# Windowed attention and SwiGLU on one core: the first query and key loads regrouped, one store per output tile, one PSUM ring

## The chip, the core and the metric

The kernel runs on one core of a Trainium2 chip. The core has a matrix engine (PE, with its weight loads listed as PEld), three engines for elementwise work (DVE, ACT and POOL), a queue engine (SP) that issues most transfers, and 16 DMA engines. The metric is device microseconds (us) of one launch; smaller is better.

## What is computed

Four batches of eight heads, 768 positions, 64 values per head. Three heads (0, 2, 6) attend to all earlier positions; the other five attend to the first four positions and to the last 64. The attention output, 3072 rows of 512, then goes through a SwiGLU block of width 1536.

```python
scores = scale * np.matmul(q, k.transpose(0, 1, 3, 2))
stream_keep = causal & (is_sink | in_win)
mask = np.where(retr, full_mask, stream_mask)
a = softmax(np.where(mask, scores, -1e9))
x = np.matmul(a, v).transpose(0, 2, 1, 3).reshape(B * S, H * D)
g = x @ w_gate
silu = g * (1.0 / (1.0 + np.exp(-g)))
out = (silu * (x @ w_val)) @ w_out
```

All inputs and the output are float32 in HBM. The kernel casts to float16 on the core and accumulates in float32.

## The kernel before, in words

**Tiles and pairs.** The 3072 rows are 24 tiles of 128 rows. Two neighbouring tiles of a batch are a pair, so there are 12 pairs; `QP` (L150) puts pair 0 of batch 0 and pair 0 of batch 1 first, and these are pairs 0 and 1 of the kernel. For each pair, `load` (L316) brings q, k and v ("x") of 256 rows and all heads as one transfer of 512 KB into a buffer of the ring `raw`: partition p holds rows 2p and 2p+1 of every head, so one contiguous run in HBM is 2 x 64 x 4 = 512 bytes. The weights come the same way in 18 transfers of 512 KB, in runs of 1 KB (gate and value) or 2 KB (output).

**Queries and keys.** `cast` (L382) makes float16 copies in the ring `hq`. For pairs 0 to 4, `transposes` (L415) turns them on PE and `evac` (L423) copies the result from PSUM to `qT` and `kT`; later pairs use a DMA transpose (`dmat`, L408). Within a tile, queries and keys stand with the 64 even rows first and the 64 odd rows after them.

**Attention of a tile.** `scores` (L484) fills a two-bank PSUM buffer of the ring `big` for up to 8 blocks (one unit of `plan`, L441), `exps` (L501) takes the exponential on ACT, `mask` (L510) multiplies by 0/1, `values` (L520) multiplies with v, `norm` (L529) divides. `xtranspose` (L538) turns the tile: for tiles 0 to 7 on PE, for the others by a DMA transpose on SP (L544).

**SwiGLU.** Six groups of four tiles. For each of 12 column blocks, `gate` (L683) makes the gate and the value product in ring `gv`, `tanh` (L691), `stt1` (L695) and `stt2` (L701) combine them into `h`. `outproj` (L717) makes the 512 output columns of one tile with 12 matmuls in three thirds, `oevac` (L728) copies PSUM to an SBUF buffer of ring `osb`, and `store` (L734) writes it out.

**The store.** An output tile stands in SBUF with even rows on partitions 0 to 63 and odd rows on 64 to 127. L739 views the 128 rows in HBM as [2, 64, columns], and L741 to L743 issue one transfer for each half: 64 partitions to 64 rows, 128 KB each. The last tile is cut into 384 and 128 columns, and its second half goes through ACT's queue.

**PSUM.** Eight banks, divided firmly (L167): three single banks `gv`, one `o`, two pairs `big`.

**The order.** Nothing is scheduled at run time. `Plan` (L78) collects some 1020 tasks; the strings `ORDER`, `WAYS` and `SLOTS` (L16 to L62), made beforehand by a planner, say in which order tasks are written to the engines, which engine takes a task that has a choice, and which buffer of a ring it uses. Each engine works through its own tasks in that order. The order also holds filler matmuls (`warm`, L295): ten at the beginning and, in this kernel, 6, 2 and 3 more in gaps of PE before 13 us.

Decoded, SP begins: q0, k0, k1, x0, q1, q2, k2, x1, then weights g1, g0, v1, v0. PE begins: ten fillers, transposes of q0, six fillers, of k0, two fillers, scores of tile 0, and so on; its first SwiGLU product uses g1. PE ends with the four tiles of the last group, 5.0 to 5.3.

Of the kernel before, what the change touches and what calls it, by code (L numbers as in the profile page):

```python
# [16 lines left out]
    "0306070200041I1J1Q1S1R01051K1Lxm1T1U1Vxi1W1X1f1g0A1q1r1z20211d1k1e081N1P1Mxj1Y1Z1a091o1p1w1y0C1O"  # L17
    "1h1i1j2K2Q2R1x2B2C292A2G0D2L2S2T0B1u1t0h22232U2V0g1b1c1m1n0n1s242526138q8r8s8g8h8i1v2D2E2F0y8M8N"
    "8O27280z8W8X2X2Y2f2a2b0m2I2J0F148j8k8Y8t8u8v8w8x0i8y8z8R8S8T2m2j2k2u118Z8a2Z0G2n0o108P8Q8U8V2l8b"
    "8c8d0E2H2y3435169091929596970l2W2p2q0k0I0r2z36370j17939498992M8e8f2N2O0H8l8m8n381l2c2d392e2P1F9U"  # L20
    "9V9W9Z9a9b8o8p2o3B3C3D0J3G3H1C9K9L3e3k3l2g2r2s2v2t0p0q3L3S3T9M0M1G9c9d303V3W199A9B9C3E3F333A3P9X"
    "9Y2h2w2x2i313I3Q3J3M3K3R3f3m3n9P9Q9R1A9D9E3u3v3U3X3Y9F9G9H3N3O323Z3a3b1D9S9T9N9O3r3s0s3o3z3p3c3d"
    "0T9I9JArAsAt0LAmAnAoAcAdAe0t15AfAg0u18ApAq9y9zA0AXAYAZAaAb4243444546470K3h4H4P4O0wAh3g4G4M4NA8A9"
    "AA129eA1A23q3w3t3x403yAuAv0x1HABAC0v1B4D4W4X4T4U4V0Q4w4z4x0N4K4L4IANAOAk9f4JAPAiAjAl0X4Y4Z0P3i48"
    "49A6ASATAU0eA3A4A5A70R1E9g9h9iAL4v52534Q6d3j4A4R4S4B4E4C0O0S9j9k9l9m9n4d4o4p4g4h4iAVAW414F4a4b4c"
    "4f4e0UAIAJAKAQAR4j4k4l4m4n9o9p9q4u514q4rADAE9r9t9u9v9w4yAG505E4s5455564t5O5V0W0c7A0YAFBkAHBlBLBM"
    "AwBmBOBNBPBnBo9x5WAM5N5U5T5B5C6k5D9sBpBqBrBfBgBhC9CACBCCCDC4C5C60VBT5758595A7j7rAxAy5z65AzB05R61"
    "785F5G5K5X5Y5Z5a5i5b5cBiBj606866B1B2B3B45d5e5r5s6eBsBt5H5I5L5J5M6364BuBvBwBzC05l5m5o5p5q5wC162B6"
    "B7B8B9BxBy5QBQBRBSBUBBBC5P5f5g5h5jBVBWBXC2C30Z6f6h6g6i676C6D6E696A5S0bBYBZ6lC7C85n5t5u5v5xBaBbBc"
    "BGBHBIBJBKBdBeBD6H6I5k6F6G6j5yDMDNDOCnCoCpD7D8D9DPDQ6B6J6K6L6NCxCyCzD0D1777E7FBABE6M6S6T6U6X6YCY"  # L30
    "DADB6m6x6n6y6o6pDCDDDEDHDIDJ6u736v6wCZ6O6P6Q6RCECFCGCqCrCaDKDLB5CHCJCKCL6z0dDUDFDGBFCMCO0f7l7kD2"
    "D3D40a6q6r6s7i70717274DRDSDTDVCPCQ767D7C7G7J7K7H7L7ICNCbCc6tCg6V6W7o7p7BCRCSCdCeCiCjCk6Z6a6b6cCI"
    "CTCUCfChCsCtCuCvCw7R7X7U7f7Y7Z7V7WCVCWD57a7b7nD67M7N79ClCm75E0E1E2EAEBECE3E4DqDrDsDtDuEFEGEHEIEJ"
    "EjEkElE5E6E7DvDwE8E9DxEZEa7O7P7Q7SDyDzEbEmEn7q7s7v7w7x7t7uDWDXDYDZDa80817yEeEfEg7c7d7g7e7zDbDcDd"
    "858B8C8D88898AEKELEcEdEN7T7h82838684DeDgDhDi8E8FEMEO8G8HDfEDEPEQER7m8I8J8K8LESETEhEiDjDlDmDnEEEU"
    "EVEWEXEY87FhFiFjFwFxFyFLF8F9FBCXDoDpEoEpEqFAFCFDFIFJErEtEsEuFKFMFNFOFPFQFRFEFFEvFkFlFGFHFmFnFoFc"
    "FdFeFXFYFfFgFZFuEwEyEzExF0F1F2DkFzFrFsF3F4G0FtFvG1G2G3FaFbFSFTFUF5F6F7FVFWFpFqG4G5G6G7G8G9GAGBGC"
    "GDGEGFGGGHGIGLGJGMGNGQGOGKGPGRGS"
)
WAYS = (  # L40
    "000000000000000000000000000000000000000000000000000000000000222222202202212222220200122001100100"
    "000000000000010022112212000011000000100000000000220021010100000100000210000000100000020022122000"
    "000010000000000100100000100000000022100201000010010000022000000000000220222222000000000000000002"
    "100010010000000012222200000010000000000000220012022000000000000000200001000000002202002010000001"
    "000000000010000000000000000120122000000000000000010002002222220000001000000001100000000000001002"
    "222000000000010000000000001001000000000000000000000000000000000000000000000000000000000000000000"
    "000000000000000000000000000000100001000000000000000000000000000000000000000000000000000000000000"
    "000000000100001000010000000000000000000000000000000000000000000000000000000000000000000000000000"
    "000000000000000000000000000000000000000000000000000000000000000000000000010000000000000010000000"
    "000000000000000000000000000000000000000000000000000000000100000000000000100000000000000000000000"  # L50
    "0000000000000000000000000000000000000000000000100000000000010"
)
SLOTS = (
    "0013427562C075931CADB91402567AB9387CD98D834BA1AB6D4285601010010000211011320215122041300240120012"
    "010121051403120120010110402000100513021113401100411020021304001012001511110402101302420100105141"
    "110100213020514011040021015030100511020411310012131200341300140211105020102100311041005120011021"
    "020321020111210100111021222002110002122410015011281112B1020A000291001701126000100012111F1100J012"
    "1H0121M000210011L2021K0021E2010C2101I1121D0000G01000101211091120N10128011261021A1110300110002140"
    "01051121B1100720002000101012010L1112C0000I0111M0011D0101H0122G1020J1002E012012002F2001K000000011"
    "102811120111060012N20217001190012A011222010B001142100521013010101011112C1010D2010I2110L2011E0110"  # L60
    "12011G1102M1100F0022J2021H1122K001100110"
# [57 lines left out]
def kernel(  # L119
# [13 lines left out]
    nc = tc.nc  # L133
# [34 lines left out]
             "h": 2 * NJ, "osb": 2, "gv": 3, "o": 1, "big": 2}  # L168
# [7 lines left out]
    for r in ("raw", "hq", "e", "xb", "xt", "sig", "sil", "h", "osb"):  # L176
        pools[r] = ctx.enter_context(tc.tile_pool(name="p_" + r, bufs=1))
    for r in ("gv", "o", "big"):
        pools[r] = ctx.enter_context(tc.tile_pool(name="ps_" + r, bufs=1, space=PSUM))
# [3 lines left out]
    def buf(ring, shape, dt, name):  # L183
        return pools[ring].tile(shape, dt, name=name, tag=ring + running[-1].slots[ring])
# [92 lines left out]
    kT = [const.tile([128, NT, 2, 2, 128], FH, name=f"kT{n}") for n in range(2)]  # L277
    QB = 3
    qT = [const.tile([128, 2, 2, 2, 128], FH, name=f"qT{n}") for n in range(QB)]
# [35 lines left out]

    def load(kind, n):  # L316
        r = buf("raw", [128, 1024], FP, "raw")
        landed[kind, n] = r
        if kind in "qkx":
            b, pi = QP[n]  # L320
            sl = slice(pi * 256, (pi + 1) * 256)
            nc.sync.dma_start(  # L322
                out=r.rearrange("p (h x) -> p h x", h=H),
                in_={"q": q, "k": k, "x": v}[kind][b, :, sl, :].rearrange(
                    "h (p j) d -> p h (j d)", j=2))
        elif kind == "o":
            nc.sync.dma_start(
                out=r.rearrange("p (a n) -> p a n", a=2), in_=wod[:, 2 * n:2 * n + 2, :])
        else:
            nc.sync.dma_start(  # L330
                out=r.rearrange("p (a n) -> p a n", a=4),
                in_=(wgd if kind == "g" else wvd)[:, :, n * 256:(n + 1) * 256])

    T_load, T_iss = {}, {}
    for kd, n in ([(kd, n) for n in range(NP) for kd in "qkx"]
                  + [(kd, n) for kd in "gvo" for n in range(6)]):
        T_iss[kd, n] = P.add(f"load {kd}{n}", ["SP"], (lambda kd=kd, n=n: load(kd, n)),
                             takes=["raw"])
        T_load[kd, n] = P.lands(T_iss[kd, n])
# [52 lines left out]
    def castv(n, m, j):  # L392
# [8 lines left out]
             r[m * 64:(m + 1) * 64, :, j].rearrange("p (a c e) d -> p a c e d", a=2, c=2))  # L401

# [160 lines left out]
    def tasks_of_pair(n):  # L563
# [4 lines left out]
        for kd in "qk":  # L568
            cs[kd] = []
            for x in range(2) if n < 2 else [None]:  # L570
# [14 lines left out]
        for kd in "qk":  # L585
# [10 lines left out]
            for x, ps in enumerate([slice(1, 4, 2), slice(0, 4, 2)] if n < 2 else [slice(0, 4)]):  # L596
                T_ev[n, kd].append(P.add(
                    f"ev{kd}{n}.{x}", ["ACT", "DVE"],
                    (lambda n=n, kd=kd, x=x, ps=ps: evac(n, kd, x, ps)), deps=[tr] + old))
# [3 lines left out]
    def tasks_of_tile(t):  # L603
# [3 lines left out]
        k_deps = [x for kt in range(i // 2 + 1) for x in T_ev[QP.index((b, kt)), "k"]]  # L607
        k_deps += T_ev[n, "q"]
# [8 lines left out]
        for u, unit in enumerate(units):  # L617
# [4 lines left out]
                       deps=k_deps + k_sinks + added, takes=["big"])  # L622
# [51 lines left out]

    for n in range(NP):
        tasks_of_pair(n)
        tasks_of_tile(2 * n)
        tasks_of_tile(2 * n + 1)
# [29 lines left out]
    def pieces(g, tt):  # L708
# [4 lines left out]
        if tt < SIZES[g] - 1:  # L713
            return [(("o", "big", "big")[tt], 0, DM)]
# [11 lines left out]
    T_oe = {}  # L726
# [7 lines left out]
    def store(g, tt, x):  # L734
# [5 lines left out]
        final = g == NG - 1 and tt == SIZES[g] - 1  # L740
        for j in range(2):  # L741
            eng = nc.scalar if j and final else nc.sync
            eng.dma_start(out=rows[j], in_=o_sbs[g, tt][j * 64:(j + 1) * 64, lo:hi])  # L743

    for g in range(NG):
# [29 lines left out]
        for tt in range(SIZES[g]):  # L775
            stores = []
            for x, (ring, lo, hi) in enumerate(pieces(g, tt)):
                for third in range(3) if x == 0 else [0]:
# [9 lines left out]
                    for j in range(js.start, js.stop):  # L788
# [5 lines left out]
                st = P.add(f"st{g}.{tt}.{x}", ["SP"], (lambda g=g, tt=tt, x=x: store(g, tt, x)),  # L794
                           deps=[oe], after=stores[:1])
# [45 lines left out]
```

## Time and profile before

| what | value |
|---|---|
| median of 3 runs | 257.44 us (255.44 to 258.09) |
| profiled execution | 254.62 us, its span 252.8 us |
| PE busy | 242.1 us, 96% of the span |
| DVE, ACT, POOL busy | 161.5, 133.9, 90.1 us |
| granted PE clock, mean | 0.997 |
| DMA, whole span | 40.72 MB, mean 161 GB/s |
| first score matmul of queries and keys | 9.27 us |
| first SwiGLU matmul | 21.62 us |
| last matmul ends | about 248.6 us |

The span runs from the first to the last instruction of the profiled execution; 1.8 us of its time lie outside it. In the groups of the profile [...]groups of matmuls add up by their busy time, not by count times mean. "DMA share" is the mean busy share of the 16 DMA engines; it exceeds 1 where packets overlap on an engine.

### The profile page before, as it was taken

To read this page: it belongs to the slowest core of one execution; us is meant where nothing else is said; L and a number is where in the kernel's file an instruction comes from. 1 tells how busy PE (TensorE), PEld (TensorE's weight loads), DVE (VectorE), ACT (ScalarE), POOL (GpSimd) and SP (SyncE) were. 2 spreads that over 40 slices of the span, in tenths; PEclk is the share of its full clock that TensorE was granted. 3 is DMA by queue.
4 is the path that set the end of the run, shared out by engine and by line. 5 is a ranking of instruction groups with operands and counts; after the bars stand their busy time and mean duration, and the time that the engine had idled before them with its cause. 6 is when DMAs were issued, how large, how long until landed. Compare 5 with 4: busy or idle time off the path is not lost.

```text
span 252.8 us, 5192 instructions
## 1 busy us (share of the span) xinstructions
PE 242.1 (96%) x2009; PEld 124.7 (49%) x2009; DVE 161.5 (64%) x291; ACT 133.9 (53%) x212; POOL 90.1 (36%) x118
## 2 busy tenths in 40 slices
PE   7987999999999979999999999999999999999993
PEld 3566755654545534444555445544455544444442
DVE  2666888877877654866887655676863556563610
ACT  3666888867686415768445843664354411232010
POOL 7376889965291703810650230500134100000000
PEclk9999999999999999999999999999999999999998
DMA  6999999999996988996954757441014131114133
GB/s 182 290 308 334 319 334 315 330 324 178 325 290 142 231 184 211 207 180 133 187 66 87 208 145 93 96 87 19 0 28 68 35 83 41 41 33 95 41 85 85
DMA packets 73369, 40.72 MB, mean 161 GB/s; under 512 B 25600, under 2 KB 68864, under 8 KB 73344
## 3 DMA queue, kind: packets, MB, share of 16 engines
q1 hardware_dynamic: 73184, 40.25, 69.1%
q8 instruction: 16, 0.26, 0.4%
q10 hardware_dynamic: 160, 0.13, 0.2%
q14 instruction: 9, 0.07, 0.1%
HBM read 28.31 MB, written 6.29 MB: 137 GB/s over the span
## 4 chain that ended last, share of the span: by engine, by line
PE 79%; DMA 8%; SPq 6%; POOL 3%; issue 1%; DVE 1%; ACT 1%; ACTq 0%; POOLq 0%; DVEq 0%
PE gv L687 46%; PE o_ps L722 22%; PE sc L499 5%; SPq L322 4%; PE av L526 4%; DMA raw<-in_moe_w_gate_dram 3%; DMA xt<-xb 3%; DMA qT<-hq 2%; POOL wg_sb L192 1%; SPq L743 1%; PE xtr L550 1%; PE tr L420 1%; DVE xb L534 1%; POOL e L516 1%; ACT sig L693 0%
## 5 line engine op out<-in xcount | busy, mean ns | idle before, releaser
L507 ACT ACTIVATE e<-sc 128x1024 f16<-128x1024 f32 (+2 forms) x68 | 59.5, 907 | 31.0 <-PE sc L499 29.1
L697 DVE SCALAR_TENSOR_TENSOR sil<-sig,gv 128x512 f32<-128x512 f32 (+1 forms) x76 | 49.8, 657 | 36.4 <-ACT sig L693 35.2
L687 PE MATMUL gv<-xt,wg_sb 128*128 128x512 f16 (+1 forms) x304 | 70.8, 368 | 1.7 <-POOL wg_sb L192 1.4
L687 PE MATMUL gv<-xt,wv_sb 128*128 128x512 f16 (+1 forms) x304 | 71.5, 368 | 0.5 <-POOL wv_sb L192 0.4
L693 ACT ACTIVATE sig<-gv 128x512 f32<-128x512 f32 (+1 forms) x76 | 43.3, 576 | 53.0 <-PE gv L687 52.3
L722 PE MATMUL o_ps<-wo_sb,h 128*128 128x512 f16 (+2 forms) x300 | 67.0, 371 | 0.0
L704 DVE SCALAR_TENSOR_TENSOR h<-sil,gv 128x512 f16<-128x512 f32 (+1 forms) x76 | 49.2, 656 | 16.7 <-PE gv L687 14.6
L516 POOL TENSOR_TENSOR e<-e,m 128x640 f16<-128x640 f16 (+1 forms) x16 | 28.2, 1769 | 44.5 <-ACT e L507 44.2
L722 PEld LDWEIGHTS <-h 128*128 128x128 f16 x300 | 28.2, 98 | 31.8 <-issue 0.2
L687 PEld LDWEIGHTS <-wv_sb 128*128 128x128 f16 x304 | 28.4, 98 | 31.0 <-POOL wv_sb L192 0.5
L687 PEld LDWEIGHTS <-wg_sb 128*128 128x128 f16 x304 | 27.7, 98 | 30.5 <-POOL wg_sb L192 1.7
L192 POOL CAST vt<-raw 64x512 f16<-64x512 f32 x30 | 19.7, 659 | 28.2 <-DMA raw<-in_v_dram 26.9
L499 PE MATMUL sc<-qT,kT 64*128 64x128 f16 x472 | 21.8, 218 | 1.8 <-DMA qT<-hq 1.7
L499 PEld LDWEIGHTS <-kT 64*128 64x128 f16 x472 | 14.4, 94 | 16.7 <-issue 15.5
L526 PEld LDWEIGHTS <-e 128*128 128x128 f16 x472 | 17.0, 97 | 5.0 <-issue 1.1
L516 DVE TENSOR_TENSOR e<-e,m 128x1024 f16<-128x1024 f16 (+1 forms) x22 | 14.3, 648 | 7.8 <-ACT e L507 7.5
L190 ACT COPY o_sb<-o_ps 128x512 f32<-128x512 f32 (+1 forms) x14 | 8.1, 578 | 21.0 <-PE o_ps L722 19.2
L526 PE MATMUL av<-vt,e 128*128 128x65 f16 x472 | 18.2, 193 | 0.5 <-POOL vt L192 0.2
L192 POOL CAST hq<-raw 128x1024 f16<-128x1024 f32 (+1 forms) x17 | 16.4, 972 | 5.0 <-DMA raw<-in_q_dram 3.3
L534 DVE TENSOR_TENSOR xb<-av,rc 128x512 f16<-128x512 f32 x24 | 16.6, 691 | 1.5 <-DMA xt<-xb 0.7
L192 DVE COPY o_sb<-o_ps 128x512 f32<-128x512 f32 (+1 forms) x11 | 7.2, 651 | 13.0 <-PE o_ps L722 13.0
L192 POOL COPY vt<-vt 2x330 f16<-2x330 f16 x10 | 4.5, 452 | 19.9 <-PE av L526 19.5
(42 smaller groups left out, 111.9 us busy)
## 6 DMA issues: line engine op xcount, KB each, us to landing
raw<-in_q_dram SPq DMA_DIRECT2D x12, 512.0 KB, 7.3
raw<-in_k_dram SPq DMA_DIRECT2D x12, 512.0 KB, 7.2
raw<-in_v_dram SPq DMA_DIRECT2D x12, 512.0 KB, 7.2
out_dram<-o_sb SPq DMA_DIRECT2D x46, 128.0 KB, 2.4
raw<-in_moe_w_gate_dram SPq DMA_DIRECT2D x6, 512.0 KB, 8.3
raw<-in_moe_w_val_dram SPq DMA_DIRECT2D x6, 512.0 KB, 8.1
raw<-in_moe_w_out_dram SPq DMA_DIRECT2D x6, 512.0 KB, 6.2
xt<-xb SPq DMA_TRANSPOSE x16, 2.8
```

Source lines behind the costliest of these rows:

```text
L192: ENG[task.way].tensor_copy(out=dst, in_=src)
L322: nc.sync.dma_start(out=r.rearrange("p (h x) -> p h x", h=H), in_={"q": q, "k": k, "x": v}[kind][b, :, sl, :].rearrange("h (p j) d -> p h ...
L499: nc.tensor.matmul(sc[:, c:c + n, :], weights, moving, start=first, stop=last)
L507: nc.scalar.activation(out=e[:, at], in_=whole_sc.pop((t, u))[:, at], func=AF.Exp, scale=scale)
L516: ENG[task().way].tensor_tensor(out=ev, in0=ev, in1=mm, op=ALU.mult)
L526: nc.tensor.matmul(avs[t][:, odd, n * 66:n * 66 + 65], ee, vv, start=(m == 0), stop=(m == len(bl) - 1))
L534: nc.vector.tensor_tensor(out=xb.rearrange("p n o d -> p o n d"), in0=av[:, :, :, 0:64], in1=rc.to_broadcast([128, 2, 4, 64]), op=ALU.mult)
L687: nc.tensor.matmul(ps, wsb[:, kk, j * 128:(j + 1) * 128], xt[:, kk, c[0]:c[1]], start=(kk == 0), stop=(kk == 3))
L693: nc.scalar.activation(out=sg[g, j, c], in_=gs[g, j, c], func=AF.Tanh, scale=0.5)
L697: nc.vector.scalar_tensor_tensor(out=sl[g, j, c], in0=sg.pop((g, j, c)), scalar=1.0, op0=ALU.add, in1=gs.pop((g, j, c)), op1=ALU.mult)
L704: nc.vector.scalar_tensor_tensor(out=hs[g, j][:, c[0]:c[1]], in0=sl.pop((g, j, c)), scalar=0.5, op0=ALU.mult, in1=vs.pop((g, j, c)), op1=A ...
L722: nc.tensor.matmul(o_open[g, tt, x], hs[g, j][:, tt * 128:(tt + 1) * 128], wo_sb[:, j, lo:hi], start=(j == 0), stop=(j == NJ - 1))
```

## The change

It does five things.

1. Queries and keys of pairs 0 and 1 come in eight transfers of 256 KB (`load_odds`), four with the odd heads first, then four with the even heads. Each fills 32 partitions: q0 on partitions 0 to 31, k0 on 32 to 63, q1 on 64 to 95, k1 on 96 to 127. A partition holds 8 rows of a head, a run of 2 KB. All four share the buffers 0 to 3 of `raw`.
2. One cast then takes a pair of heads of all four tensors at once (`cast4`, four casts of 1024 columns instead of eight of 512), `transposes4` turns it with 8 transposes, as many in all as before, and `evac4` copies it in two parts, one for each pair of tiles. A score unit waits only for the heads that it uses.
3. `store` issues one transfer for a tile, with the HBM side [2, 64, columns] and the SBUF side [128, columns]. It may go through SP's or ACT's queue. `osb` has three buffers.
4. The eight PSUM banks are one space; a slot number names a bank, and a `big` buffer takes two neighbouring ones. `raw` and `hq` are each one tensor that is cut into slots.
5. The order, the engines and the slots are planned anew. There are no fillers after the first ten.

Decoded from the new strings, SP begins: k1, q0, k0, q1 (odd heads), k0, q0, q1, k1 (even heads), x0, k2, q2, x1, v0, g0, g1, v1. PE begins: ten fillers, the transposes of the odd heads (`tr4.3`, `tr4.2`), of the even heads, score units 1.0, 0.0, 1.1, 3.0, 2.0; its first SwiGLU product uses v0, after `xe0` and `xe1`. PE ends: out 4.1, four products of group 5 and value and gate products, out 4.2, the first third of out 4.3, out 5.0, 5.1, 5.2, 5.3 (384 columns, then 128), the last two thirds of out 4.3. The last stores are 4.1 (ACT), 4.2, 5.0, 5.1 (SP), 5.2 (ACT), 5.3 in two parts (SP, ACT) and 4.3 (ACT). Around 80 to 110 us SP holds: xdma8, dq7, xdma9, load q9, dk6, load k8, stores 0.1 and 0.2, load k7, dq8.0, xdma10, store 1.0, xdma11, dk7, with store 0.0 on ACT's queue ("xdma" turns a finished tile, "dq" and "dk" are the DMA transposes of queries and keys).

```diff
     RINGS = {"raw": 14, "hq": 5, "e": 6, "xb": 3, "xt": 2, "sig": 2, "sil": 3,
-             "h": 2 * NJ, "osb": 2, "gv": 3, "o": 1, "big": 2}
+             "h": 2 * NJ, "osb": 3, "ps": 8, "gv": 8, "o": 8, "big": 8}
...
-    for r in ("gv", "o", "big"):
-        pools[r] = ctx.enter_context(tc.tile_pool(name="ps_" + r, bufs=1, space=PSUM))
+    banks = [psum.tile([128, 1024], FP, name=f"banks{x}") for x in range(4)]
+    rooms = {"raw": const.tile([128, RINGS["raw"], 1024], FP, name="rooms_raw"),
+             "hq": const.tile([128, RINGS["hq"], 1024], FH, name="rooms_hq")}
...
+    def load_odds(kind, n, odd):
+        b, pi = QP[n]
+        at = 64 * n + 32 * "qk".index(kind)
+        nc.sync.dma_start(
+            out=rooms["raw"][at:at + 32, 0:4].rearrange("p a b -> p (a b)").rearrange(
+                "p (h o x) -> p h o x", o=2, x=512)[:, :, odd],
+            in_={"q": q, "k": k}[kind][b, :, pi * 256:(pi + 1) * 256, :].rearrange(
+                "(h o) (p j) d -> p h o (j d)", o=2, j=8)[:, :, odd])
...
+    def cast4(p):
+        src = rooms["raw"][:, 0:4].rearrange("p a b -> p (a b)").rearrange(
+            "p (k s r j d) -> p k s r j d", k=2, s=2, r=2, d=64)
+        hqs[p] = buf("hq", [128, 1024], FH, "hq")
+        recast(T_c4[p], hqs[p].rearrange("p (j s d) -> p s j d", s=2, d=64),
+               src[:, p % 2, :, p // 2])
+
+    def transposes4(p):
+        tr = trs[p] = buf("gv", [128, 8, 128], FH, "tr")
+        for j in range(8):
+            nc.tensor.transpose(
+                tr[:, :, j * 16:j * 16 + 16],
+                hqs[p][:, j * 128:(j + 1) * 128], ident)
+
+    def evac4(p, x):
+        at = p % 2 * 256 + p // 2 * 128
+        dst = qkT[:, 2 * x:2 * x + 2, 0:1024].rearrange("c g (m n) -> c g m n", m=2)
+        copy(T_e4[p, x], dst[:, :, :, at:at + 128].rearrange(
+                 "c g m (i n l) -> c g m i n l", i=2, l=4),
+             trs[p].rearrange("c (x g m) (l i n) -> c x g m i n l", x=2, g=2, i=2, l=4)[:, x])
...
         rows = out[r0:r0 + 128, lo:hi].rearrange("(p j) n -> j p n", j=2)
-        final = g == NG - 1 and tt == SIZES[g] - 1
-        for j in range(2):
-            eng = nc.scalar if j and final else nc.sync
-            eng.dma_start(out=rows[j], in_=o_sbs[g, tt][j * 64:(j + 1) * 64, lo:hi])
+        eng = nc.scalar if T_st[g, tt, x].way == "ACT" else nc.sync
+        eng.dma_start(out=rows, in_=o_sbs[g, tt][:, lo:hi])
```

## The prediction, made before the result was known

> **What bounds the kernel now.** First the page: its head, the slices of PE and DMA, and the chain of waits by line.
>
> ```profile
> span 252.8 us, 5192 instructions
> ...
> PE   7987999999999979999999999999999999999993
> ...
> DMA  6999999999996988996954757441014131114133
> ...
> PE gv L687 46%; PE o_ps L722 22%; PE sc L499 5%; SPq L322 4%; PE av L526 4%; DMA raw<-in_moe_w_gate_dram 3%; DMA xt<-xb 3%; DMA qT<-hq 2%; POOL wg_sb L192 1%; SPq L743 1%; PE xtr L550 1%; PE tr L420 1%; DVE xb L534 1%; POOL e L516 1%; ACT sig L693 0%
> ```
>
> PE is full from about 25 us to the end. So the end is: when PE gets full, plus the matmuls left, plus PE's gaps, plus what follows the last matmul. How much gap there is says the table of windows; its columns are PE, PEld, DVE, ACT, POOL busy, clock, DMA share, GB/s.
>
> ```profile
> 25.50:238.00 212.50, 210.03 (x1705) 106.45 (x1705) 145.83 (x251) 117.47 (x189) 74.22 (x82) 1.00 0.68 152
> ```
>
> 2.5 us are idle in the middle; no more can be won there, save on switches between kinds of matmul. The list of waits names for PE only small ones, none on an engine that empties PSUM:
>
> ```profile
> PE sc L499 <- DMA qT<-hq: 1.7, 2, 1.5
> ...
> PE gv L687 <- POOL wg_sb L192: 1.4, 1, 1.4
> ```
>
> Then the chain in order of time, for when PE gets full and for the end:
>
> ```profile
> 12.01 8.39 DMA raw<-in_moe_w_gate_dram
> 20.45 0.08 issue
> 20.53 1.05 POOL wg_sb L192
> 21.57 0.05 issue
> 21.62 1.05 PE gv L687 x8
> ...
> 238.21 10.40 PE o_ps L722 x60
> ...
> 248.64 0.29 DVE o_sb L192
> ```
>
> The first SwiGLU product waits for the ninth 512 KB load (g1), which lands at 20.45. The load stream sets this, as one-microsecond windows show:
>
> ```profile
> 10.00:11.00 1.00, 1.00 (x18) 0.60 (x16) 0.73 (x2) 1.00 (x2) 0.57 (x1) 1.00 1.19 289
> ...
> 17.00:18.00 1.00, 1.00 (x19) 0.83 (x19) 0.23 (x3) 1.00 (x2) 0.30 (x1) 1.00 1.15 345
> ```
>
> DMA is saturated in both: at 289 GB/s with 512-byte runs (q, k, v), at 345 with 1 KB runs (weights). The stores, from the table of transfers and half-microsecond windows of the tail:
>
> ```profile
> out_dram<-o_sb SPq DMA_DIRECT2D x46, 128.0 KB, 2.4
> ```
>
> ```profile
> 245.00:245.50 0.50, 0.50 (x4) 0.25 (x3) 0.00 (x0) 0.00 (x0) 0.00 (x0) 1.00 0.46 111
> 245.50:246.00 0.50, 0.50 (x5) 0.21 (x3) 0.00 (x0) 0.00 (x0) 0.00 (x0) 1.00 1.02 229
> 246.00:246.50 0.50, 0.50 (x5) 0.30 (x4) 0.00 (x0) 0.44 (x1) 0.00 (x0) 1.00 0.83 188
> ```
>
> A tile of 256 KB (two transfers) leaves in about 1.2 us over 16 engines, and each transfer lands 2.4 us after its issue.
>
> [...]a tile stored by two 64-partition transfers averages 262 KB / 1.2 us, about 215 GB/s, though single windows are above it. [...]The trace shows the half clock at the beginning (fillers 0.43 us apart until 5.67, then 0.22) and keeps PE busy afterwards.
>
> **Change 1 and 2, the start.** 2.1 MB of q and k now pass at 290 GB/s: 7.2 us. If run length decides, they pass at 347 (weights): 6.0 us, a gain of 1.2. [...]I take 215, since eight transfers queue without gaps: 9.8 us, a loss of 2.5. v0 has the ninth place that g1 had, so it lands at 20.45 + 2.5 = 23.0; its half cast takes 0.6 instead of 1.05, and the first product starts at 23.7, 2.1 later.
>
> The attention chain must be no later. Data flows from 2.4 us on; the odd half (1.05 MB) lands at 2.4 + 4.9 + 0.9 (what q0 took beyond its flow) = 8.2, the even half at 13.1. Cast of 1024 columns on ACT or POOL 1.1, transposes of two casts 1.1, two evacuations on ACT 2 x 0.58, scores 0.4: unit 0.0 is done at 16.9 (before: 9.9). Then ACT has ex0.0, ex1.1, ex3.0, ex2.0 (4 x 1.03), evk2 (1.02), ex3.1 (1.03), xe0 and xe1 (0.4 each), which ends at 23.9, when PE may start vals0.0. Both chains say 24, against 21.6: +2.4. The casts (4 x 1.04 for 8 x 0.62) and evacuations (8 for 8) save 0.8 us of engine time under the load stream: nothing. Evacuations read PSUM in strides, which no row shows: 0 to 0.4 us each, two on the chain; I take 0.
>
> Eleven fillers go (about 2.9 us of PE, in gaps): no gain. Without them PE idles from 5.7 to about 9.4. If the clock halves, score units take 0.8 instead of 0.4[...]; I take 0.3. Start: **+2.7**, from -1.6 to +4.5.
>
> **Change 3, the store.** HBM [2, 64, 512] has slowest dimension 2, SBUF [128, 512] has 128[...]: each of two engines moves 131,072 bytes, where it moved 16,384. No row shows a single engine alone. [...]from above: the saturated weight stream, 347 / 16 = 21.7 GB/s, 6.0 us. I take 5.3 us, an estimate. All stores, of both queues, share these two engines. Counting from PE's end E, with 0.86 us for four matmuls of 512 columns and 0.6 for the copy, stores are issued at -12.4 (4.2), -8.9 (5.0), -6.3 (5.1), -3.7 (5.2), and the data starts 1.2 later (before: the last ones issued at 248.95, bytes from about 250.1). 4.2 flows until -5.9; from there the two engines are never free: 5.0 until -0.6, 5.1 until 4.7, 5.2 until 10.0, 5.3 (192 and 64 KB) until 15.3, 4.3 until 20.6. The copy of 4.3 also waits for its `osb` buffer until 5.1 has landed, about 6, which is early enough. The span ends 1.5 after the last byte (before: 251.3 to 252.8): 22.1 instead of 252.8 - 248.6 = 4.2. Tail: **+18**, from +13[...] to +22 (6.0). The 25 issues that are saved (about 0.6 us each) lie on SP, which waits for copies there (55 us before L743 in the list of SP's waits): nothing; were SP late, it would be up to 15 us of earlier loads.
>
> Middle: between 80 and 160 us DMA packets take this share of the 16 engines (the table of transfers of that window):
>
> ```profile
> q1 hardware_dynamic: 30969, 12.54, 79.9%
> ```
>
> That is 64 us of 80, perhaps 53 without overlap (saturation showed 1.2). Eight stores add 8 x 5.3 = 42 us to two engines, and every load and transpose needs all 16: 95 to 106 us of work in 80. xdma10 and xdma11 stand on SP behind stores 0.1, 0.2 and 1.0, and gate2.0 waits for them; dk7 after them feeds tile 14. On ACT's queue stand store 0.0 and, behind it, a cast and exponentials of tile 10[...]. The late transposes cost PE between 0 (slack hides it) and 26; from 160 us on the DMA share is 0.23, and it recovers. I take **+6**.
>
> **Change 4 and 5.** PE waits for no PSUM buffer now, so the common ring gives at most part of the 2.5 us idle: -1 to 0, taken as 0. One tensor for all slots could bring waits where slots overlap in the tracking; nothing in the code makes them overlap in bytes: 0. The third `osb` buffer is spent on late stores.
>
> **Sum.** 254.6 + 2.7 + 18 + 6 = 281.3 against the profiled execution. The median of the runs shown is 257.4, 2.8 higher; so half of that is added: 283.
>
> **Rivals.** (A) The main case[...]: 283; its own range 266 to 303. (B) A transfer is divided by its bytes, not by its outermost dimension: the store spreads over 16 engines, and only the slow start counts: the last store is one of 256 KB after a copy of 0.58, some 0.7 later than now; 254.6 + 2.7 + 0.7 - 1 = 257, up to 261 with the median's excess. For it: nothing in the trace[...]. (C) The other side, faster: as B for the stores, and run length, not partitions, decides the rate of the eight quad loads. Place: the load stream until v0; price: -1.2 at 347 GB/s and -0.45 for the shorter cast, with ring and order up to -2.5: 250 to 254. For it: the trace's own step from 289 to 345 GB/s with longer runs. It decides from 290 GB/s on, where the start stops being later. Even then it wins only while a store lands fast: PE makes the last tiles 2.6 us apart, so from 2.6 us per store on the tail piles up, and 5.3 is twice that.
>
> **Chances.** A 0.70, B 0.13, C 0.14, others 0.03. About 1% is what a measurement of this kernel can tell. A is slower; B is half within 1%, a third slower; C is faster: faster 0.17, same 0.09, slower 0.74. Range: A up to 299 (0.65), B (0.12) and C's upper end (0.04) from 253 on.
>
> **What would show it.** A: DMA share near 2/16 with some 40 to 55 GB/s after the last matmul, 18 us of it; issue to landing of a store 7 us or more; landings of xdma10 and xdma11 above 8 us; PE gaps at 90 to 160. B: windows of 200 GB/s and less in the first 12 us, v0's product after 23 us, and a tail of 5. C: over 300 GB/s from the first quad on. Wrong altogether if score units start before 10 us and stores land within 3.

## The result and the profile after

| kernel | median, us | range, us | ratio to before [95% interval] |
|---|---|---|---|
| before | 256.97 (4 runs) | 255.44 to 258.09 | |
| after | 415.46 (4 runs) | 414.54 to 416.11 | 1.617 [1.608, 1.627] |

The change costs 158.5 us. Medians here and below are over all executions; the ratios leave out the few that ran more than 1.5% slower than the fastest of the same kernel. The forecast was 283 us with a range up to 299: the sign was right, the size far too small. The profiled execution took 414.99 us, its span 413.2. First the same rows of the page as before: head, busy times, the slices of PE, its clock and DMA, and the chain by line.

```profile
span 413.2 us, 5149 instructions
...
PE 278.8 (67%) x1998; PEld 136.2 (33%) x1998; DVE 168.7 (41%) x282; ACT 141.5 (34%) x218; POOL 88.1 (21%) x117
...
PE   5867668765678974689757747654948786679710
...
PEclk9599979988889978899998996989896999788975
DMA  8999995062049979157995084100175100000111
...
PE banks L774 30%; DMA out_dram<-o_sb 12%; PE banks L809 9%; DVE sil L784 8%; DVE h L791 7%; ACT sig L780 5%; PE banks L580 3%; ACT e L588 3%; PE banks L607 2%; DMA rooms_raw<-in_k_dram 2%; DMA xt<-xb 2%; SPq L490 1%; ACT o_sb L211 1%; DVE xb L615 1%; DVE e L597 1%
```

PE was full and is now idle for a third of the span, from end to end and not just in the middle or the tail. It also has more busy time (278.8 against 242.1 us) for fewer matmuls: its clock is granted only in part (mean 0.887, before 0.997), and each matmul lasts longer (a gate product 403 ns on average in its group, 368 before). Of the 160.4 us by which the span grew, 36.7 are such busy time; the rest is waiting. New links stand in the chain: `sil`, `h` and `sig`, DVE's and ACT's work on a SwiGLU block, on which PE did not wait before. The list of waits (total, times, longest) says the same:

```profile
PE banks L774 <- DVE sil L784: 38.3, 29, 3.1
...
PE banks L774 <- DVE h L791: 28.6, 21, 3.6
...
ACT o_sb L211 <- DMA out_dram<-o_sb: 23.0, 3, 9.6
...
DVE o_sb L213 <- DMA out_dram<-o_sb: 12.9, 3, 6.7
```

Two groups: SwiGLU products wait for the engines that empty PSUM, and the copies of the output wait for stores. The first group comes earlier than any store. The first store is issued at 128.6 us, but the windows (PE, PEld, DVE, ACT, POOL busy, clock, DMA share, GB/s) show PE at 73% from 40 us on:

```profile
40.00:80.00 40.00, 29.21 (x309) 16.42 (x309) 24.58 (x44) 19.34 (x31) 15.11 (x20) 0.91 0.73 216
100.00:120.00 20.00, 14.56 (x64) 5.67 (x63) 9.69 (x17) 7.67 (x12) 2.12 (x1) 0.83 0.07 12
```

In the second row even DMA is idle (12 GB/s), and no engine is full: a chain of waits, not an engine, sets the pace. The timeline shows one link of it:

```profile
43.49 0.68 DVE L784 SCALAR_TENSOR_TENSOR sil<-sig,banks 128x512 f32<-128x512 f32 x1
...
44.22 1.02 PE L774 MATMUL banks<-xt,wg_sb 128*128 128x512 f16 x4 [1.57 <-DVE sil L784]
```

The four matmuls write bank 0; the DVE instruction that they wait for reads bank 1, decoded from the slots. The two banks have nothing in common but the tensor: the change cuts PSUM into four tensors of two banks each.

The tail is close to the forecast. After the last matmuls only stores run, at a DMA share near 2/16 and 51 GB/s:

```profile
396.00:400.00 4.00, 0.00 (x0) 0.00 (x0) 0.00 (x0) 0.00 (x0) 0.00 (x0) 0.75 0.13 51
404.00:408.00 4.00, 0.00 (x0) 0.00 (x0) 0.00 (x0) 0.00 (x0) 0.00 (x0) 0.50 0.14 49
```

A share of 0.13 to 0.14 is 2.1 to 2.2 of 16 engines. If two engines carry the stores, an estimate from this share, 51 GB/s are 25.5 GB/s an engine, and 262,144 bytes take 5.15 us (forecast: 5.3). The stores of both queues share this rate: one issued on SP at 384.69 us and one on ACT at 387.45 landed together, at 401.7 and 401.9.

### The profile page after: what moved, and what is told of

Its sections match the earlier page's. It is cut to its first block, busy times and chain, and to the rows that moved or that the text cites. A ratio compares the mean times of both kernels' runs of the same rounds, so it can differ in the third digit from the quotient of the medians.

```text
span 413.2 us, 5149 instructions
## 1 busy us (share of the span) xinstructions
PE 278.8 (67%) x1998; PEld 136.2 (33%) x1998; DVE 168.7 (41%) x282; ACT 141.5 (34%) x218; POOL 88.1 (21%) x117
## 4 chain that ended last, share of the span: by engine, by line
PE 46%; DVE 18%; DMA 16%; ACT 10%; issue 4%; SPq 2%; POOL 1%; ACTq 0%; DVEq 0%; POOLq 0%
PE banks L774 30%; DMA out_dram<-o_sb 12%; PE banks L809 9%; DVE sil L784 8%; DVE h L791 7%; ACT sig L780 5%; PE banks L580 3%; ACT e L588 3%; PE banks L607 2%; DMA rooms_raw<-in_k_dram 2%; DMA xt<-xb 2%; SPq L490 1%; ACT o_sb L211 1%; DVE xb L615 1%; DVE e L597 1%
## 5 line engine op out<-in xcount | busy, mean ns | idle before, releaser
L774 PE MATMUL banks<-xt,wg_sb 128*128 128x512 f16 (+1 forms) x304 | 82.2, 403 | 49.4 <-DVE sil L784 22.6
L774 PE MATMUL banks<-xt,wv_sb 128*128 128x512 f16 (+1 forms) x304 | 80.5, 398 | 37.6 <-DVE sil L784 15.7
L780 ACT ACTIVATE sig<-banks 128x512 f32<-128x512 f32 (+1 forms) x76 | 43.4, 575 | 139.3 <-PE banks L774 127.7
L784 DVE SCALAR_TENSOR_TENSOR sil<-sig,banks 128x512 f32<-128x512 f32 (+1 forms) x76 | 49.6, 659 | 84.6 <-ACT sig L780 78.4
L809 PE MATMUL banks<-wo_sb,h 128*128 128x512 f16 (+2 forms) x300 | 73.0, 398 | 15.8 <-DVE h L791 6.0
L588 ACT ACTIVATE e<-banks 128x1024 f16<-128x1024 f32 (+2 forms) x68 | 58.9, 910 | 44.9 <-PE banks L580 34.4
L791 DVE SCALAR_TENSOR_TENSOR h<-sil,banks 128x512 f16<-128x512 f32 (+1 forms) x76 | 49.9, 658 | 46.7 <-PE banks L774 38.1
L597 POOL TENSOR_TENSOR e<-e,m 128x1024 f16<-128x1024 f16 (+1 forms) x17 | 32.8, 1935 | 131.6 <-ACT e L588 131.3
L580 PE MATMUL banks<-qkT 64*128 64x128 f16 x472 | 21.6, 230 | 0.0
L607 PE MATMUL banks<-vt,e 128*128 128x65 f16 x472 | 20.1, 200 | 2.1 <-DVE vt L217 1.6
L213 POOL CAST rooms_hq<-rooms_raw 128x1024 f16<-128x1024 f32 x13 | 13.8, 1060 | 25.5 <-DMA rooms_raw<-in_k_dram 13.2
```

Of the source, the lines that this page charges most:

```text
L213: ENG[task.way].tensor_copy(out=dst, in_=src)
L580: nc.tensor.matmul(sc[:, c:c + n, :], weights, moving, start=first, stop=last)
L588: nc.scalar.activation(out=e[:, at], in_=whole_sc.pop((t, u))[:, at], func=AF.Exp, scale=scale)
L597: ENG[task().way].tensor_tensor(out=ev, in0=ev, in1=mm, op=ALU.mult)
L607: nc.tensor.matmul(avs[t][:, odd, n * 66:n * 66 + 65], ee, vv, start=(m == 0), stop=(m == len(bl) - 1))
L774: nc.tensor.matmul(ps, wsb[:, kk, j * 128:(j + 1) * 128], xt[:, kk, c[0]:c[1]], start=(kk == 0), stop=(kk == 3))
```

## The experiments

The theory after the result: the loss is the sum of (P) waits between neighbouring banks of one PSUM tensor, (S) the store on two engines, and a small rest from the start. The rivals: only one of the two; or the new order itself. "Both" below means that the edits are made together. All medians stand beside runs of the kernel before on the same chip (254.7 to 255.4 us).

| run | edit | median, us | ratio to before [95%] |
|---|---|---|---|
| b_pairs | before, four two-bank tensors | 355.13 | 1.395 [1.389, 1.402] |
| t_half | before, two four-bank tensors | 570.63 | 2.229 [2.212, 2.245] |
| b_one | before, one eight-bank tensor | 254.88 | 1.001 [0.997, 1.004] |
| a_banks | after, eight one-bank tensors | 317.08 | 1.245 [1.241, 1.250] |
| a_one | after, one eight-bank tensor | 313.35 | 1.227 [1.221, 1.233] |
| a_store | after, two stores a tile | 376.95 | 1.482 [1.475, 1.489] |
| a_both | a_banks and a_store | 259.91 | 1.018 [1.012, 1.025] |
| b_store | before, one store a tile | 315.28 | 1.238 [1.233, 1.242] |
| b_store_osb6 | b_store, six output buffers | 300.81 | 1.179 [1.172, 1.186] |
| b_tail | b_store in the last group only | 269.08 | 1.055 [1.050, 1.060] |
| b_mid | b_store in groups 0 to 4 only | 301.03 | 1.182 [1.176, 1.189] |
| b_store16 | before, one store to 128 rows in a row | 251.51 | 0.987 [0.984, 0.990] |
| b_nat | b_store16 with strided moving operands | 404.30 | 1.583 [1.576, 1.591] |
| a_fixed | a_one and the edit of b_nat | 404.80 | 1.586 [1.578, 1.594] |
| b_order | b_store16, rows put in order by DVE | 252.28 | 0.990 [0.987, 0.993] |
| a_order | a_one and the edit of b_order | 256.29 | 1.003 [1.000, 1.005] |
| a_warm | a_order with fillers in the start | 257.00 | 1.008 [1.005, 1.011] |

**PSUM alone, in the kernel before (b_pairs).** Every bank keeps its number; only the tensors are made differently.

```diff
-        pools[r] = ctx.enter_context(tc.tile_pool(name="ps_" + r, bufs=1, space=PSUM))
+    banks = [psum.tile([128, 1024], FP, name=f"banks{x}") for x in range(4)]
...
+            room = banks[at // 2][:, at % 2 * 512:(at % 2 + wide) * 512]
```

> The kernel before; its PSUM buffers keep their banks and their order, but the three gv banks and the o bank are cut out of two tensors of two banks (gv0 with gv1, gv2 with o); each big pair is a tensor as it was. Theory (waits are set for a whole PSUM tensor, so neighbours in one tensor wait for each other): PE waits before products for the reader of the neighbouring bank; slower by 40 to 120 us, the granted clock below 0.95. Rival (the loss comes from the stores or from the new order): within 3 us of before.

It costs 100 us, and the new waits are those of the changed kernel. The granted clock fell less than expected (0.974 in the profiled execution). From the list of waits of this run:

```profile
PE banks L703 <- DVE sil L713: 37.0, 37, 2.3
```

**Is it any shared tensor? (b_one, t_half.)** The same kernel with one tensor of eight banks, then with two of four.

```diff
+    banks = [psum.tile([128, 4096], FP, name=f"banks{x}") for x in range(1)]   # b_one
+    banks = [psum.tile([128, 2048], FP, name=f"banks{x}") for x in range(2)]   # t_half
```

> The kernel before with all eight PSUM banks in one tensor; banks, slots and order unchanged. Theory (a wait is set for any two accesses of one tensor, whatever bank): far slower than with pairs, 420 us and more, since then scores, products and output products exclude each other too. Rival (only the neighbouring bank of a pair counts): about the 355 of pairs.

This missed altogether: one tensor costs nothing. So "a wait for any two accesses of one tensor" fell, and t_half asked whether a larger tensor is harmless or only one that holds all eight banks.

> The kernel before, with its eight banks as two tensors of four banks each (bank numbers unchanged). Theory (waits for neighbouring banks in a tensor of two or four banks): at least as slow as with four tensors of two banks, 355 us; I expect 360 to 450, and waits of PE for the readers in nearly every product. Rival (it is the placing of the buffers in pairs, not the size of the tensor, and a larger tensor is harmless as one of eight banks was): 254 to 257.

Four banks in a tensor are far worse than two: 570.6 us. The list of waits again names the readers:

```profile
PE banks L703 <- DVE sil L713: 69.8, 48, 2.7
...
PE banks L703 <- DVE h L720: 33.4, 40, 2.3
```

With two or four banks in a tensor (355.13 and 570.63 us) a write to one waits for a reader of another; with all eight in one (254.88 us) it does not. The kernels b_pairs, t_half and b_one give every buffer the same bank number and differ only in the tensor that holds it. So which bank a buffer has does not decide, and the waits are most likely set when the program is built; that is argued from these three runs, not read from its instructions. Why a tensor of all eight banks is free of them stays open.

**PSUM and stores undone in the changed kernel (a_banks, a_one, a_store, a_both).** a_banks gives each bank its own tensor, and so cuts the exponentials and the division of `norm` at the bank border; a_one only makes one tensor of the four. a_store issues two transfers a tile, as before.

```diff
-    banks = [psum.tile([128, 1024], FP, name=f"banks{x}") for x in range(4)]
+    banks = psum.tile([128, 4096], FP, name="banks")            # a_one
...
-        eng.dma_start(out=rows, in_=o_sbs[g, tt][:, lo:hi])     # a_store
+        for j in range(2):
+            eng.dma_start(out=rows[j], in_=o_sbs[g, tt][j * 64:(j + 1) * 64, lo:hi])
```

> The changed kernel with each PSUM bank a tensor of its own; an exponential over two banks and the division become two instructions each. Stores as changed. Theory (whole-tensor waits): PE idles little again, 275 to 295 us, which is the store's tail plus the later start. Rival (the new order itself is bad, or the stores are): above 350.

> The changed kernel with its eight PSUM banks as one tensor instead of four tensors of two banks; the store stays one transfer over two engines. Theory (the slow part of the PSUM change is the two-bank tensor, in which a write of one bank waits for a reader of the other; one tensor of eight banks has no such waits): 310 to 325 us, as with a tensor for each bank. Rival (in this kernel, with its buffers spread over all banks, one tensor brings neighbours' waits too): 410 or more.

> The changed kernel with two stores of 64 partitions per tile again, on the queue that the plan names. Theory (PSUM tensors are the main cost, stores only the tail and some waits for output buffers): 415 minus 22 to 45 us, 370 to 393. Rival (stores on two engines are the main cost): 250 to 290.

> The changed kernel with each PSUM bank a tensor of its own (exponentials and divisions in two instructions) and two stores of 64 partitions per tile. What is left of the change: the regrouped loads, the later start without fillers, the new order. Theory (PSUM tensors and stores are all of the loss): 252 to 264 us. Rival (the new order costs by itself): 270 and more.

Either way of mending PSUM gains about 100 us (98.4 and 102.1), as much as b_pairs lost. Two stores gain 38.5 while PSUM is slow and 57.2 once it isn't (317.08 to 259.91): some 19 us are lost as long as either cause is there, so a slow kernel hides part of the late stores. With both, 4.8 us above before are left. a_banks missed its range, since the store's cost was still thought smaller than it is.

**The store alone, in the kernel before (b_store).**

```diff
-        for j in range(2):
-            eng = nc.scalar if j and final else nc.sync
-            eng.dma_start(out=rows[j], in_=o_sbs[g, tt][j * 64:(j + 1) * 64, lo:hi])
+        nc.sync.dma_start(out=rows, in_=o_sbs[g, tt][:, lo:hi])
```

> The kernel before with one store per tile, [2, 64, columns] against [128, columns], all on SP; nothing else. Theory (two engines per store, 5.15 us for 256 KB at 51 GB/s): the tail grows by 16 to 20 us and late transposes cost 0 to 6: 273 to 283 us. Rival (the stores also cause the losses of the middle): 330 us and more.

It costs 60.6 us, over twice what the theory (and the prediction, 24) gave it, and less than the 75 of the rival. The list of waits shows full output buffers:

```profile
ACT o_sb L190 <- DMA out_dram<-o_sb: 49.7, 10, 9.7
...
DVE o_sb L192 <- DMA out_dram<-o_sb: 30.7, 7, 9.5
```

Were these buffers the reason, more of them should win most of it back.

```diff
-             "h": 2 * NJ, "osb": 2, "gv": 3, "o": 1, "big": 2}
+             "h": 2 * NJ, "osb": 6, "gv": 3, "o": 1, "big": 2}
```

> The kernel before with one store per tile, and six output buffers in place of two. Theory (of the 60 us of one store per tile some 40 are copies that stand on ACT and DVE until a slow store gives its buffer back): 272 to 285 us, of which the tail is 18 to 22. Rival (the middle is lost to transposes that are late behind stores on two DMA engines): 300 and more.

They win back 14.5 us, and the waits for stores shrink to one:

```profile
ACT o_sb L190 <- DMA out_dram<-o_sb: 8.2, 1, 8.2
```

Yet the time stays at 300.8. The chain in order of time of that run (start, duration) shows what is late instead: loads and DMA transposes behind the stores.

```profile
113.54 8.94 DMA raw<-in_k_dram
...
147.24 9.31 DMA kT<-hq
...
161.93 9.60 DMA raw<-in_q_dram
...
185.79 10.43 DMA xt<-xb
```

The table of transfers of the kernel before has these medians from issue to landing:

```profile
raw<-in_k_dram SPq DMA_DIRECT2D x12, 512.0 KB, 7.2
...
xt<-xb SPq DMA_TRANSPOSE x16, 2.8
kT<-hq SPq DMA_TRANSPOSE x14, 3.5
```

So the transposes are late above all.

**By stage (b_tail, b_mid).** One transfer for the last group only, or for all groups but the last.

```diff
+        if g == NG - 1:        # b_mid: g < NG - 1
+            nc.sync.dma_start(out=rows, in_=o_sbs[g, tt][:, lo:hi])
+            return
```

> The kernel before; only the four tiles of the last group leave in one transfer over two engines (on SP), the other twenty in two halves as before. Theory (the tail alone): +18 us, 270 to 276. Rival (a good part of what the single stores cost came later through the loads and transposes only, and the tail hides behind the last matmuls): 256 to 265.

> The kernel before; the twenty tiles of groups 0 to 4 leave in one transfer over two engines, the four of the last group in two halves as before. Theory (single stores cost 60.6 us in all, of which 18 are the tail; the rest is late transposes and loads and full output buffers in the middle, and the terms add): 293 to 300. Step of the prediction (middle +6, at most 26): 257 to 281.

The tail costs 14.3 us, the middle 46.2, and together 60.5 they are the whole of b_store. Both runs lie 1 us outside the range of their theory (270 to 276, 293 to 300), and the 257 to 281 that the prediction's step gave b_mid are far off. The windows of b_mid show where:

```profile
80.00:100.00 20.00, 14.82 (x147) 7.71 (x146) 9.16 (x14) 5.66 (x10) 4.96 (x5) 0.96 1.24 158
...
120.00:140.00 20.00, 16.25 (x122) 7.99 (x121) 11.22 (x20) 11.26 (x18) 3.91 (x4) 0.83 0.89 128
...
180.00:200.00 20.00, 11.74 (x93) 5.41 (x91) 6.76 (x13) 7.02 (x12) 2.82 (x5) 0.85 0.61 66
```

and the kernel before in the last of them:

```profile
180.00:200.00 20.00, 20.00 (x192) 10.39 (x191) 11.33 (x21) 8.75 (x12) 7.28 (x8) 1.00 0.22 41
```

PE loses 8.3 us of 20 there while the mean DMA share is 0.61 and only 66 GB/s pass. Single DMA engines are not seen in the profile, but the traces have the semaphore events of the transfers. The kernel before has 2,368 for 148 transfers, half stores among them, 16 for each; the changed kernel has 1,707, which are 16 for each of 102 loads and transposes and 3 for each of 25 stores. Of the three of the store issued at 384.69 us one came at 385.62 and two at the end, at 401.58 and 401.71. With a share of 0.13 to 0.14 in the tail this reads as transfers that need all sixteen engines and wait for the two that the stores keep busy; that is argued from these counts, no engine was seen by itself. The stores hold up the output too: over the run the copies of ACT and DVE stand 39.8 and 21.9 us for output buffers. And 12.5 us of the 46.2 are longer busy time of PE (254.6 against 242.1 us), at a mean clock of 0.951.

**Is it the outermost dimension? (b_store16.)** One store again, but to 128 rows in a row, so that both sides have 128 outermost.

```diff
-        rows = out[r0:r0 + 128, lo:hi].rearrange("(p j) n -> j p n", j=2)
+        rows = out[r0:r0 + 128, lo:hi]
```

> The kernel before with one store per tile, but from 128 partitions straight to 128 rows of HBM, so both sides have an outermost dimension of 128. The same bytes in the same 128 runs of 2 KB; even and odd rows of a tile are left out of order in the output. Theory (the outermost dimension of 2 confines a store to two engines): 253 to 258 us, as before, and a store of 256 KB at 200 GB/s and more. Rival (one store of 256 KB is slow as such): 300 and more.

251.5 us, 1.3% faster than before, a gain that was not expected and whose cause is open. The transfers land 2.2 us after their issue, no later than the halves did (2.4), and a window of the tail moves 303 GB/s where the halves reached 229:

```profile
245.00:245.50 0.50, 0.50 (x7) 0.34 (x5) 0.00 (x0) 0.00 (x0) 0.00 (x0) 1.00 0.79 303
```

So one transfer of 256 KB over 128 partitions is harmless; the 2 in front was it.

**A version that keeps the order (b_nat, a_fixed, b_order, a_order).** The first try made the gate and value products read x in natural row order, in steps of 128 bytes.

```diff
-                ps, wsb[:, kk, j * 128:(j + 1) * 128], xt[:, kk, c[0]:c[1]],
+                ps, wsb[:, kk, j * 128:(j + 1) * 128],
+                xt[:, kk, c[0]:c[1]].rearrange("p (t j n) -> p t n j", j=2, n=64),
```

> The kernel before with one store for each tile over 128 partitions and 128 consecutive rows, and the gate and value products reading the turned x in natural row order (every 64th column after the other, in steps of 128 bytes), so that the output stands in natural order. Theory (the outermost dimension decides the engines of a store, and PE reads a moving operand at the same rate in any order): 250 to 254, as with the rows left in their order (251.5). Rival (strided moving operands are slower): the gate and value products, 60% of PE, take up to twice their time, up to 400.

> The changed kernel with both causes mended and the rest kept: one PSUM tensor of eight banks, and one store for each tile over 128 consecutive rows, with the products reading x in natural order. Theory (PSUM tensors and the store's two engines are all of the loss but some 3 to 5 us of the start): 254 to 260. Rival (strided moving operands are slower): as for the kernel before with this edit, up to 400.

The rival held in both. The group of gate products of b_nat (busy, mean ns):

```profile
L687 PE MATMUL gv<-xt,wg_sb 128*128 128x512 f16 (+1 forms) x304 | 147.8, 620 | 1.5 <-POOL wg_sb L192 1.5
```

It was 70.8 us before: twice the time for the same matmuls. The second try leaves PE alone; the last product on DVE, `stt2`, is cut into even and odd rows and writes every second column.

```diff
+        for odd in range(2):
+            nc.vector.scalar_tensor_tensor(
+                out=hs[g, j][:, c[0]:c[1]].rearrange("p (t n j) -> p j t n", j=2, n=64)[:, odd],
+                in0=s_.rearrange("p (t j n) -> p j t n", j=2, n=64)[:, odd],
...
+        rows = out[r0:r0 + 128, lo:hi]
```

> The kernel before with one store for each tile over 128 consecutive rows, the rows put in natural order by the last SwiGLU product of DVE, which is cut into two of 256 columns for even and odd rows and writes every second column. Theory (the store on 16 engines gains some 3 us; the second instruction costs DVE about 0.06 us in each of 76, hidden behind PE; writing every second column costs DVE nothing): 250 to 255. Rival (strided columns slow DVE to half rate, 0.66 us more in each of 76: DVE would have 212 us of work in 252 and PE waits for h): 257 to 275.

> The changed kernel with both causes mended in the same way: one PSUM tensor of eight banks, and one store for each tile over 128 consecutive rows, with the rows put in order by two products of DVE. Theory (PSUM tensors and the store's two engines are all of the loss but 3 to 5 us of the start): 254 to 261. Rival (something else in the plan costs, hidden so far): above 263.

Both hit. `stt2` costs DVE 6 us more in all, hidden behind PE (the group of b_order; before: 76 with a mean of 656 ns, 49.2 us in all):

```profile
L706 DVE SCALAR_TENSOR_TENSOR h<-sil,gv 128x256 f16<-128x256 f32 (+1 forms) x152 | 55.3, 423 | 16.1 <-PE gv L687 14.0
```

b_order is the fastest version that keeps the row order, 1.0% below the kernel before; the changed kernel with both causes mended is level with before (interval 1.000 to 1.005).

**The start (a_warm).** a_order has no fillers after the first ten, and its clock is halved (0.50 from 10 to 18 us) while PE waits for the loads and in the transposes and scores after them. a_warm puts 13 ahead of the transposes of each half.

```diff
+        if p in (3, 1):
+            warm(13)
         tr = trs[p] = buf("gv", [128, 8, 128], FH, "tr")
```

> The changed kernel with both causes mended (as in the run before, 256.3 us), and 13 filler matmuls put back on PE ahead of each of the two pairs of transposes of the start, while PE waits for the loads of the odd and of the even heads. Theory (half a clock from 9 to 19 us costs part of the 4 us that the start is later): the clock stays at 1.0, the transposes and scores of the start take half of their time, and the whole is 0.5 to 2 us faster, 254.3 to 255.8. Rival (loads and exponentials set the start, PE's clock doesn't matter): 256 to 257.

The clock does what the theory says. The window from 14 to 16 us in a_order, then in a_warm:

```profile
14.00:16.00 2.00, 2.00 (x17) 1.55 (x14) 0.04 (x1) 1.17 (x2) 1.51 (x5) 0.50 1.19 290
```

```profile
14.00:16.00 2.00, 2.00 (x32) 1.39 (x31) 0.64 (x2) 1.60 (x3) 1.59 (x5) 1.00 1.20 290
```

32 matmuls instead of 17 in the same time, and the first SwiGLU product starts at 24.29 us instead of 25.72. The total doesn't follow: 257.0 us. From 26 to 32 us PE of a_warm has a gap of 0.7 us where a_order has none, so half of the early gain of 1.4 us is gone. The other half lasts: of an exponential on the chain of both, a_warm's starts at 86.84 us and a_order's at 87.44. Then it is lost, and more: PE of a_warm is idle 1.8 us longer between 80 and 100, where its chain has a DMA transpose that a_order's has not (why it is late there is open):

```profile
92.59 5.12 DMA qkT<-rooms_hq
```

What follows the start is set by other things than PE's clock there. The rival held.

## Why the prediction was wrong, step by step

**Change 4: the step that failed.** It priced one tensor for all slots with "nothing in the code makes them overlap in bytes: 0". The bytes do not overlap; the waits are there all the same, for the bank beside it in a two-bank tensor. The step looked at the one thing that it named as a danger, "waits where slots overlap in the tracking", and priced it by the bytes alone. Measured: +100.4 us (b_pairs, 355.13 less 254.7), and -98 to -102 when undone in the changed kernel, where it is over 60% of the whole loss. `raw` and `hq`, made into one tensor each by the same step, stay so in a_order, which is level with before; there the 0 was right, or nearly. The trace of before could not show it, since each of its PSUM buffers was a tensor of its own; what could have been asked is what PE would wait for if neighbouring banks were coupled, and that was no small number: in the kernel before PE fills one bank while DVE reads another (a value product of 61.53 to 62.56 us beside a `sil` of 61.50 to 62.19), and PE's list of waits names no engine that empties PSUM; in b_pairs, with the same banks, PE waits 37.0 us for `sil` alone. Different banks are not enough when they belong to one two-bank tensor.

**Middle: right mechanism, wrong size.** "+6", at most 26; measured +46.2 (b_mid), the largest mis-sized term of the store. Two assumptions failed. The estimate stopped at 160 us, where "it recovers", since the mean DMA share is low; but a mean over 16 engines can hide two that are full (as read from the event counts above), and b_mid lost 8.3 us between 180 and 200. And "slack hides it" as the lower end: PE of the kernel before had none, being 98% busy from 80 to 160 us (78.25 of 80) and full from 180 to 200. Output buffers, priced at nothing beside the third one, carry 14.5 us of b_store (which has two).

**Tail: right mechanism, size within its range.** Two engines a store were the author's assumption, 5.3 us a tile an estimate, and the low end of +13 had nothing in the trace behind it. Measured in the changed kernel: a share of 0.13 to 0.14, which is 2.1 to 2.2 of 16 engines, 3 semaphore events a store where the halves had 16, and about 51 GB/s within the forecast 40 to 55, so 5.15 us a tile. The last matmul ends at 393.94 us, and the span 19.3 us later, where 22.1 were forecast: +15 instead of +18. The difference is a wait of PE just before its end (the timeline):

```profile
391.52 0.65 ACT L211 COPY o_sb<-banks 128x384 f32<-128x384 f32 x2 [6.85 <-DMA out_dram<-o_sb]
392.05 1.89 PE L809 MATMUL banks<-wo_sb,h 128*128 128x512 f16 x8 [2.80 <-ACT o_sb L211]
```

The copy waited for a store to give back its buffer, and the last eight matmuls for the copy, which reads the bank beside theirs. Without these 2.8 us the two would be 22.1 apart. In the kernel before the same kind of tail costs 14.3 (b_tail), with four tiles behind each other where the new order has six.

**Start: near, and it hardly matters.** Forecast: odd halves landed at 8.2, even at 13.1, at 215 GB/s, the author's estimate (the prediction reads the same rate for a tile's two half stores). Measured in the changed kernel: casts start at 7.54 and 12.13, the loads of 256 KB pass at 188 to 264, mostly 219 to 256 GB/s. The first product comes 4.1 us later than before in a_order, against 2.1 to 2.4 forecast; 1.4 of the rest is the half clock (a_warm), which the prediction gave 0.3. In the changed kernel the clock was halved some 3.2 us after the last filler ended (at 8.9 against 5.7) and full again with the scores at 19 us. The strided copies out of PSUM, bounded at 0 to 0.4 us each, cost nothing on ACT (0.59 us for 512 columns, against the 0.58 that the forecast took); five of the eight ran on DVE, and there they took 0.68 us, where 512 columns took 0.42 before.

**What is left: start, ring and order.** With both causes mended the changed kernel is 3 to 4 us slower than the kernel before with the same mending (ratios to before 1.003 and 0.990; medians 256.29 and 252.28). The two profiled executions differ by only 2.0 us: PE ends 1.5 later (250.19 against 248.68) and what follows is 0.5 longer. That is less because b_order's profiled execution took 253.59 us, 1.3 more than its median, with half the clock from 22 to 25 us, and a_order's 255.60, 0.7 less. How the rest divides between start, ring and order was not tried; a_warm shows that the half clock isn't it.

**The sum.** Undone one after the other in the changed kernel, the causes add up: 98.4 (PSUM: 415.46 to 317.08), then 57.2 (stores: to 259.91), and 2.9 of start and order down to the 256.97 of before make 158.5. Apart, in the kernel before, they cost 100.4 and 60.6. The sign was no luck, since stores and start alone make the kernel some 60 us slower; over 60% of the size come from the step priced at 0. Rival B (stores spread, 257) and C fell with the tail at 2/16. The error of form lay in the range: it was built from stores and loads, with no case in which PSUM waits appear. (The upper ends of the main case, +4.5, +22 and +26, reach 307 and not its 303; that changes nothing here.)

## What to carry to other kernels

When buffers are merged into larger tensors, ask how waits are set between parts of one tensor, and price a coupling of neighbours from the profile of before; it was the largest term here (some 100 us), from a line that was meant to change nothing. Look at the outermost dimension of both sides of every transfer: a 2 in front held the stores of the tail at 51 GB/s and a DMA share of 0.13, two engines of 16 as this case reads it, and its price was less its own 5 us than what stood behind it, transposes and copies that wait for output buffers, even where the mean DMA share was low. A gain at the start of PE's stream is one only if what comes next is limited by PE: a_warm had its first product 1.4 us earlier and ended at 257.00 us against 256.29.

## What the runs showed of the hardware that was not expected

- A moving operand read in steps of 128 bytes took twice the time: 147.8 us for 304 matmuls against 70.8 (b_nat). DVE, writing every second float16 column, showed no such price: its instructions of 256 columns, with some shorter ones among them, took 423 ns on average in b_order, and one of 256 unbroken columns 418 in the kernel before, so the 55.3 us against 49.2 are nearly all the cost of 76 more instructions.
- Eight transfers of 256 KB to 32 partitions each, queued one behind another on four different sets of partitions, passed at about 233 GB/s (2.1 MB in the 9 us from 2 to 11), above the 215 that the prediction took and below the 290 of the 512 KB loads of queries, keys and values in the kernel before (5 to 15 us). What share of this the runs of 2 KB, the 32 partitions and the change between partitions have was not tried.
- One store of 256 KB over 128 rows in a row reached 303 GB/s in a window of half a microsecond (b_store16); two of 64 partitions reached 229 (the kernel before).
- A DMA share of 1.24 went with only 158 GB/s (b_mid, 80 to 100 us), where the kernel before moved 278 at 1.14 (40 to 80 us): so the share seems to count packets that wait as well as packets that move; this was not tried by itself.
